# One fused kernel of a linear recurrence and an MLP: a new order of its steps on every queue, half-length MLP pieces, and two chunk results from one product

## The chip, the cores and the metric

The kernel runs on one core of a Trainium2 chip. A core has five engines that run side by side, each with an in-order instruction queue: TensorE (PE, matrix products; its weight loads are listed apart as PEld), VectorE (DVE), ScalarE (ACT), GpSimd (POOL) and SyncE (SP), which here does nothing but issue DMAs. They wait for one another by semaphores. Matrix products read SBUF and write PSUM, which is here a pool of four tiles of two banks each ("duo" in the code). The metric is the time of one execution on the device in microseconds (us).

## What is computed

The reference is a recurrence over 768 time steps for 4 batches x 8 heads with a 40 x 40 state each, and then a two-layer MLP with exact GELU over the 3072 tokens:

```python
for t in range(S):                      # S = 768
    y[:, :, t] = einsum('bhd,bhde->bhe', rt, state)
    Sa = einsum('bhde,bhe->bhd', state, at)
    state = state * wt[:, :, None, :] - einsum('bhd,bhe->bhde', Sa, bt) \
            + einsum('bhd,bhe->bhde', vt, kt)
x = y.transpose(0, 2, 1, 3).reshape(3072, 320)
out = gelu(x @ w_in) @ w_out            # w_in 320 x 2048, w_out 2048 x 320
```

All is in float32, except that the MLP's weights arrive as 64-bit floats and have to be turned into 32-bit ones on the chip, from their two 32-bit words.

## The kernel before, in words

**Chunks.** The 768 steps are cut into 12 chunks of 64 (c = 0 to 11). Within a chunk the recurrence becomes products of 64 x 64 blocks per head. With the decay of w taken into a and r (as running products) and out of b and k (as their inverses), the strictly upper parts are taken of four products: N = b.a, A = k.a, RV = v.r, and later M = sa.r. The inverse of the triangular system with N gives T (stored in `Tt`). Then, with the state S at the chunk's start:

- `make_av` (L640): av = A x v, copied to SBUF by ACT; `make_X` (L808): X = a x S, to which DVE adds av (L819).
- `make_sa` (L821): sa = T x (X + av), 40 columns per head, copied into `SM`; `make_saT` (L833): the same transposed, copied by ACT (L842, L843); `make_M` (L846): M = sa x r, masked by DVE (L575) into the other 64 columns of `SM`.
- `make_y2` (L850): r x S into the PSUM tiles `QY`, from the transposed state that `turn_state` (L912) makes; `make_QY` (L870): b x [sa | M] and k x [v | RV] added there, 104 columns at once.
- `outputs` (L879): DVE scales the 64 columns of y into `xt` (L886), adds and scales the new state (L908, L909), and SP moves parts of `xt` between partitions by eleven small DMAs (L894, L897), because 40 rows of a head don't fill 64 partitions.

Each of these steps is 32 products of a quarter of PE's array (`units`, L588), written by the helper `mm` (L110), so one line stands for all of them in the profile. A float32 product is two instructions: 32 products are x64 in a view.

**The inverse** of a chunk is made a chunk ahead. N goes to DRAM (L615) and comes back in another layout (`Nb`, L664); POOL eliminates column by column, 31 columns of a product (L672, tile `tmp`) and an addition (L674, tile `W`); the result goes to DRAM (L686, issued by POOL) and is fetched into `Tt` and `T2` (L696, L700). `corner` (L774) and `joined` (L789) put the 64 x 64 inverse together from its 32 x 32 blocks, with DVE's transpose `L` (L772) and copies of J. Chunk 0 takes another way, squarings on PE (`squares`, L712).

**Loads.** r, k, v, w, a, b of a chunk come by `fetch`, `fetch_pairs`, `load_w`, `load_r` and `load_VR` (L159 to L223), nearly all on SP's queue. For late chunks DVE's 32 x 32 transposes (L186) turn a, b, k, v and r. SP issues in program order and waits at each DMA whose buffer is in use.

**The MLP** of a chunk (`mlp`, L985) is a generator. Up to each `yield` it is one piece: four pieces of the first layer (`ph`, 20 products of 64 x 128 tiles, then a GELU by ACT at L995), and then the second layer (`po`): for chunks 0 and 1 four pieces at L1010, for later chunks four pieces of `seven` (L936), which takes seven block products in place of eight, with DVE's sums. `fill()` (L1024) takes the next piece of the oldest MLP in the list `pieces`, so the program text decides between which steps of the chunks the MLP's work stands on PE.

**The weights' conversion** (`to_float`, L312) is a handful of instructions of DVE (L319 to L328), ACT (L320) and, for some pieces, POOL (L332, L333): 10 pieces of w_in of 512 columns and 16 of w_out of 320. `first_load` and `second_load` bring the words into places that are free at that time; `convert(n)` (L338) begins the next n pieces of one queue and ends the ones before.

**The order** is written by hand: straight text for chunks 0 and 1 and the preparation of 2 and 3 (L1059 to L1242), then a loop over c = 2 to 11 (L1244) in which chunk c runs, c + 1 is prepared and c + 2 is loaded and its inverse begun. `keep(n)` puts idle products (identity times a mask, n x 128 columns) ahead of the next PSUM tile's real ones.

Of the kernel before, what the change touches and what calls it, by code (L numbers as in the profile page):

```python
# [19 lines left out]
def kernel(  # L20
# [193 lines left out]
    def load_VR(c):  # L214
        VR = turned_in.setdefault(c, {})["VR"] = VR_ring()
        for e in range(2):
            nc.sync.dma_start(out=VR[half(e)].rearrange("p g q m d -> p (g q m) d")[:, :, :D], in_=rows_of(v, c, e))
# [20 lines left out]
    st_ring = ring("st", 1, [P, 2, NP, G, HP], lambda t: t.rearrange("p e i g d -> p (e i g) d")[:, :, D:], nc.gpsimd)  # L238
# [34 lines left out]
    upper = const.tile([P, C], FP32, name="upper")  # L273
# [15 lines left out]
    part_ring, avs_ring = (ring(n, 1, [P, 2, DM + REST], lambda t: t[:, :, DM:], nc.gpsimd) for n in ("part", "avs"))  # L289
# [46 lines left out]
    queue, begun = [], []  # L336

    def convert(n, last=False):  # L338

        for _ in range(n):  # L340
            begun.append(queue.pop(0))
            next(begun[-1], None)
            if len(begun) > 1:
                next(begun.pop(0), None)
        if last:
            while begun:
                next(begun.pop(0), None)

    first_raw, second_raw = {}, {}
    late_raw = w_out_sb.rearrange("p f d -> p (f d)").bitcast(UINT32)  # L350
# [59 lines left out]
    def first_pieces(kts, part, eng):  # L410
        queue.extend(first_convert(kt, part, eng) for kt in kts)

    def second_pieces(fs, eng):
        queue.extend(second_convert(f, eng) for f in fs)
# [6 lines left out]
    decays, turned_in = {}, {}  # L421
# [5 lines left out]
    def sums(c):  # L427
        logw = raws.pop((c, "w"))
        pt = duo("wT_ps").rearrange("p e (n t) -> p e n t", t=C)
        for n in range(G * NP):  # L430
            for x in range(2):
                for e in range(2):
                    at = (2 * n + x) * D
                    mm(pt[half(x), e, n], logw[half(e), at:at + HP], cum_m[half(e), half(e)])
        cum = duo("cum")[:, :, :DM]
# [4 lines left out]
        wp = wp_ring()  # L440
        turned_in.setdefault(c, {})["wp"] = wp
        if c < NB:
            nc.scalar.activation(wp[:, :, 1:].rearrange("p (n e) t -> p e n t", e=2), pt, ACT.Exp)  # L443
        else:
            en = turned_in.setdefault(c, {})["en"] = by_batch(side("en", "kT", 1))
            for to, scale_ in ((wp[:, :, 1:].rearrange("p (g n e) t -> p g e n t", g=G, e=2), 1.0),
                               (en.rearrange("p (e g n) t -> p g e n t", e=2, g=G), -1.0)):
                for g in range(G):
                    nc.scalar.activation(to[:, g], pt[:, ::1 - 2 * g, g * NP:(g + 1) * NP], ACT.Exp, scale=scale_)
        rw = (avs_ring if c in (1, 2) else part_ring)()[:, :, :DM]  # L450
# [27 lines left out]
    def turn_a(c):  # L478
        if c < NT:
            turned_in.setdefault(c, {})["a_ps"] = flip(by_pair(raws.pop((c, "a"))), "aT_ps")  # L480
            return
        aT = turned_in.setdefault(c, {})["aT"] = work.tile([P, 2, G, NP, C], FP32, tag="aT", name="aT", bufs=2)
        turn(aT.rearrange("p e g i t -> p (e g i) t"), c, "a")
# [112 lines left out]
    direct = (0,)  # L596

    def make_N(c):
# [10 lines left out]
        if c in direct:  # L609
            return  # L610
# [8 lines left out]
    def make_RV(c, mask=True):  # L619
        t = turned_in[c]  # L620
        t["RV_ps"] = products("RV_ps", t["vT"], t["rT"], False)
        if mask:
            mask_RV(c)
# [5 lines left out]
    def make_A(c, mask=True):  # L629
        t = turned_in[c]  # L630
        t["A"] = work.tile([P, 2, G, NP, C], FP32, tag="nT", name="A")
        t["A_ps"] = products("A_ps", t["kT"], t["aT"], False)
        if mask:
            mask_A(c)
# [4 lines left out]

    def make_av(c):  # L640
        t = turned_in[c]
        av = duo("av")[:, :, :G * NP * D].rearrange("p x (g i d) -> p x g i d", g=G, i=NP)
        for g, i, x, e, q, m in units():
            mm(av[half(e ^ x), x, g, i], t["A"][half(e), x, g, i], t["VR"][half(e), g, q, m, :D])
        avs = t["avs"] = avs_ring()
        nc.scalar.copy(avs[:, :, :DM], av.rearrange("p x g i d -> p x (g i d)"))
# [161 lines left out]
    def make_X(c):  # L808
        t = turned_in[c]
        if state[0] is None:  # L810
            t["xs"] = t["avs"]
            return
        st = state[0][0]
        X = duo("X")[:, :, :G * NP * D].rearrange("p x (g i d) -> p x g i d", g=G, i=NP)
        for g, i, x, e, q, m in units():
            mm(X[half(e ^ x), x, g, i], t["aT"][half(x, D), g, i, e], st[half(x, D), e, i, g, :D])

        xs = t["xs"] = part_ring() if c == 1 else t["avs"]
        nc.vector.tensor_tensor(xs[:, :, :DM], X.rearrange("p x g i d -> p x (g i d)"), t["avs"][:, :, :DM], ALU.add)  # L819

    def make_sa(c):  # L821
        t = turned_in[c]
        xs = t["xs"]
        Tt = t["Tt"]
        sap = duo("sap")[:, :, :G * NP * D].rearrange("p x (g q a d) -> p x g q a d", g=G, q=2, a=NA)
        for g, i, x, e, q, m in units():
            at = (g * NP + i) * D
            mm(sap[half(e), x, g, q, i % NA], Tt[half(e ^ x), x, g, i], xs[half(e ^ x), x, at:at + D])
        SM = t["SM"] = SM_ring()
        copy = nc.scalar.copy if 0 < c <= NS else nc.vector.tensor_copy  # L830
        copy(SM.rearrange("p g q (a x) c -> p x (g q a) c", x=2)[:, :, :, :D], sap.rearrange("p x g q a d -> p x (g q a) d"))

    def make_saT(c):  # L833
        t = turned_in[c]
        xs, Tt = t["xs"], t["Tt"]
        pt = duo("saT_ps").rearrange("p r (i x t) -> p r i x t", i=NP, x=2)
        for g, i, x, e, q, m in units():
            at = (g * NP + i) * D
            mm(pt[half(g), e ^ x, i, x], xs[half(e ^ x), x, at:at + HP], Tt[half(e ^ x), x, g, i])
        saT = side("saT", "late", 1)  # L840
        to = saT.rearrange("p g (a x) (e t) -> p (g a) (x e) t", x=2, e=2)
        nc.scalar.copy(to[:, :, 0::3], pt[:, 0])  # L842
        nc.scalar.copy(to[:, :, 1:3], pt[:, 1])  # L843
        t["saT"] = parts(saT)

    def make_M(c):  # L846
        t = turned_in[c]
        masked(flat(t["SM"])[:, :, D:], products("M_ps", t["saT"], t["rT"], False))

    def make_y2(c):  # L850


        t = turned_in[c]
        t["QY"] = [duo("QY")[:, :, :NP * VC].rearrange("p e (i c) -> p e i c", i=NP) for g in range(G)]
        if state[0] is None:
            return
        tn = state[0][1]
        for i in range(NP):
            for e in range(2):
                for x in range(2):  # L860
                    for g in range(G):
                        mm(t["QY"][g][half(x), e, i, D:], tn[half(g, D), e, i, half(x)],
                           t["rT"][half(g, D), i // NA, 2 * (i % NA) + x, e], i == 0)
# [6 lines left out]
    def make_QY(c):  # L870
        t = turned_in[c]
        for n, (l_, r_) in enumerate(((t["nb"], t["SM"]), (t["ks"], t["VR"]))):
            for g, i, x, e, q, m in units():
                mm(t["QY"][g][half(x), e, i], columns(l_[half(e)], g, head_of(i, x)), r_[half(e), g, q, m],
                   state[0] is None and n == 0 and i == 0)
# [3 lines left out]
    def outputs(c):  # L879
# [487 lines left out]
```

## Time and profile before

| | |
|---|---|
| three runs | 714.76, 717.62, 717.79 us; median 717.62 |
| profiled execution | 722.93 us, span 721.2 us from the first to the last instruction |
| busy in the span | PE 670.3, PEld 592.0, DVE 370.7, POOL 361.1, ACT 223.0 us |
| instructions | 32844, of which PE 14826 products |
| mean granted PE clock | 0.960 |
| DMA | 74.46 MB in 287923 packets, 103 GB/s on the mean |
| first layer `ph` (L993) | 1920 instructions, 220.4 us of PE |
| second layer `po` (L946, L1010) | 1248 instructions, 201.3 us of PE |
| POOL's inverse (L672, L674) | 620 instructions, 267.5 us |

The page lists the busy time of each engine, the span in 40 equal slices (each digit is the busy share in tenths), the chain of work that ended last, and the groups of instructions by line. The trace can be asked for waits (who waited for whom), for the busy time in any stretch, and for the instructions in order of time. A busy PE is not PE at its peak: products are pipelined and their ends are modelled, so what a step costs PE is read from the start of its first product to the start of the next step's first.

### The profile page before, as it was taken

How to read it: one execution, taken by the hardware profiler on the slowest of the kernel's cores; microseconds unless marked ns; L12 is line 12 of the kernel's file. 1: busy time of each engine (PE TensorE's matmuls, PEld its weight loads, DVE VectorE, ACT ScalarE, POOL GpSimd, SP SyncE). 2: the span in 40 equal slices, each digit the busy share in tenths (PEclk: the TensorE clock that was granted, in tenths of full speed). 3: DMA queues.
4: the chain of work that ended last, by engine and by line, in shares of the span. 5: the costliest groups of instructions: out<-in, count | busy, mean ns of one | idle time of the engine just before them, and what ended most of it. 6: DMA issues, size and time to landing. Idle time of an engine off the chain costs nothing.

```text
span 721.2 us, 32844 instructions
## 1 busy us (share of the span) xinstructions
PE 670.3 (93%) x14826; PEld 592.0 (82%) x14826; DVE 370.7 (51%) x490; ACT 223.0 (31%) x311; POOL 361.1 (50%) x798
## 2 busy tenths in 40 slices
PE   7578897869999999999999999999999899999997
PEld 4567777747777889899898998898898798998987
DVE  2324889993353386384384573662761671621403
ACT  5123674444140241341332232323313323112020
POOL 5284458811841860882863844855845827800000
PEclk9775799989999999999999999999999999999999
DMA  9688437664557645757657656747737644020100
GB/s 127 119 164 153 97 87 200 132 127 96 116 115 111 131 92 90 134 101 118 130 97 132 127 92 118 140 74 128 145 62 138 132 93 73 21 54 3 28 11 18
DMA packets 287923, 74.46 MB, mean 103 GB/s; under 512 B 265736, under 2 KB 284456, under 8 KB 287784
## 3 DMA queue, kind: packets, MB, share of 16 engines
q1 hardware_dynamic: 283360, 68.20, 51.0%
q0 software_dynamic: 864, 2.36, 2.0%
q8 instruction: 116, 1.90, 1.1%
q10 hardware_dynamic: 3560, 1.80, 1.0%
q14 instruction: 23, 0.19, 0.1%
HBM read 58.69 MB, written 9.70 MB: 95 GB/s over the span
## 4 chain that ended last, share of the span: by engine, by line
PE 52%; POOL 13%; SPq 11%; DMA 10%; DVE 5%; issue 5%; ACT 3%; ACTq 1%; DVEq 0%; POOLq 0%
PE ph L993 16%; PE po L946 12%; POOL W L674 6%; POOL tmp L672 6%; PE po L1010 5%; PE QY L110 4%; PE J L110 2%; DMA Nb<-N 2%; DMA Tt<-inv 2%; DMA inv<-W 2%; SPq L181 2%; PE sq L110 2%; SPq L897 2%; SPq L178 2%; PE X L110 1%
## 5 line engine op out<-in xcount | busy, mean ns | idle before, releaser
L993 PE MATMUL ph<-xt,w_in_sb 64*128 64x256 f32 x1920 | 220.4, 381 | 0.3 <-issue 0.3
L672 POOL TENSOR_TENSOR tmp<-W,Nb 128x126 f32<-128x126 f32 (+22 forms) x310 | 131.9, 425 | 157.6 <-DMA Nb<-N 134.6
L993 PEld LDWEIGHTS ph<-xt,w_in_sb 64*128 64x128 f32 x1920 | 182.7, 187 | 23.3 <-issue 1.7
L674 POOL TENSOR_TENSOR W<-W,tmp 128x126 f32<-128x126 f32 (+22 forms) x310 | 135.6, 438 | 24.3
L995 ACT ACTIVATE gt<-ph 128x1024 f32<-128x1024 f32 x48 | 49.1, 1023 | 153.0 <-PE ph L993 152.9
L946 PE MATMUL po<-w_out_sb,gt 128*128 128x160 f32 x640 | 92.2, 302 | 0.1
L946 PEld LDWEIGHTS po<-w_out_sb,gt 128*128 128x128 f32 x640 | 87.5, 190 | 2.4 <-DVE gt L966 0.4
L186 DVE STREAM_TRANSPOSE aT<-a_pairs 128x1024 f32<-128x1024 f32 x9 | 11.2, 1246 | 62.9 <-DMA a_pairs<-in_a_dram 62.9
L1010 PE MATMUL po<-w_out_sb,gt 128*128 128x320 f32 x128 | 38.5, 459 | 2.2 <-ACT wpT L443 2.2
L1010 PEld LDWEIGHTS po<-w_out_sb,gt 128*128 128x128 f32 x128 | 25.2, 201 | 13.3 <-ACT wpT L443 2.4
L802 DVE COPY Tt<-J 32x512 f32<-32x512 f32 x9 | 6.2, 689 | 52.8 <-ACT Tt L802 52.8
L786 ACT COPY Js<-J 128x256 f32<-128x256 f32 x11 | 4.1, 370 | 88.7 <-PE J L110 88.7
L946 PE MATMUL po<-extra,half 128*128 128x160 f32 x192 | 28.5, 303 | 0.0
L998 DVE TENSOR_TENSOR half<-gt 128x1024 f32<-128x1024 f32 x10 | 12.4, 1244 | 28.0 <-ACT gt L995 28.0
L946 PEld LDWEIGHTS po<-extra,half 128*128 128x128 f32 x192 | 26.4, 190 | 0.4
L575 DVE TENSOR_TENSOR SM<-M_ps,upper 128x1024 f32<-128x1024 f32 x12 | 14.5, 1204 | 21.2 <-PE M_ps L110 21.2
L320 ACT ACTIVATE conv<-conv,rebias 128x320 uint32<-128x320 uint32 (+1 forms) x26 | 16.1, 623 | 27.8 <-DVE conv L319 22.0
L995 ACT ACT_TABLE_LOAD x10 | 12.8, 1283 | 37.2 <-PE ph L993 37.1
L946 PE MATMUL po<-extra,gt 128*128 128x160 f32 x160 | 23.4, 299 | 0.0
L946 PEld LDWEIGHTS po<-extra,gt 128*128 128x128 f32 x160 | 22.3, 190 | 0.0
L950 DVE TENSOR_TENSOR os<-os,po 128x160 f32<-128x160 f32 x40 | 12.6, 316 | 18.6 <-PE po L946 12.5
L961 ACT COPY os<-po 128x160 f32<-128x160 f32 x10 | 2.9, 292 | 59.1 <-PE po L946 50.2
(224 smaller groups left out, 1144.2 us busy)
## 6 DMA issues: line engine op xcount, KB each, us to landing
Nb<-N SPq DMA_DIRECT2D x20, 256.0 KB
VR<-in_v_dram SPq DMA_DIRECT2D x24, 160.0 KB
out_dram<-os SPq DMA_DIRECT2D x48, 80.0 KB
b_rows<-in_b_dram SPq DMA_DIRECT2D x22, 160.0 KB
k_rows<-in_k_dram SPq DMA_DIRECT2D x22, 160.0 KB
N<-N SPq DMA_DIRECT2D x44, 64.0 KB
Tt<-inv SPq DMA_DIRECT2D x44, 64.0 KB
a_pairs<-in_a_dram SPq DMA_DIRECT2D x18, 144.0 KB
```

What stands on the lines that cost most here:

```text
L110: nc.tensor.matmul(o, lhsT, rhs, start=first, stop=True, skip_group_check=True)
L178: eng.dma_start(out=to[:, e::2], in_=pairs[rows, :, cols])
L181: eng.dma_start(out=to, in_=pairs[rows, :, cols])
L320: nc.scalar.activation(power, power, ACT.Relu, bias=rebias, scale=8.0)
L575: nc.vector.tensor_tensor(to, pt, upper.unsqueeze(1).to_broadcast([P, 2 * G * NP, C]), ALU.mult)
L672: eng.tensor_tensor(t, W[:, :rows, j:j + 1].to_broadcast([P, rows, rest]), Nb[:, j:j + 1, j + 1:].to_broadcast([P, rows, rest]), ALU.mult)
L674: eng.tensor_tensor(W[:, :rows, j + 1:], W[:, :rows, j + 1:], t, ALU.add)
L897: eng.dma_start(out=xt[own + n * i:own + n * (i + 1), NP], in_=xt[other + REST:other + D, i])
L946: nc.tensor.matmul(po[:, n, :DM // 2], l_[:, f], r_[:, f], start=f == 0, stop=f == NF // 2 - 1)
L993: nc.tensor.matmul(ph[:, x, s], w_in_sb[half(x), kt, p * P:(p + 1) * P], xt[half(x), kt], start=kt == 0, stop=kt == NK - 1)
L995: nc.scalar.activation(gt[:, 4 * q:4 * q + 4].rearrange("p (x s) t -> p x s t", x=2), ph, ACT.Gelu)
L1010: nc.tensor.matmul(po[:, g], gt[:, f, g * P:(g + 1) * P], w_out_sb[:, f], start=f == 0, stop=f == NF - 1)
```

## The change

1. **sa and M from one product.** `make_av` now takes A x [v | RV] (104 columns), and `make_X` adds a x [S | y2] to it in the same PSUM tiles (`XA`), so the tile holds [X + av | its product with r]. ACT and DVE copy it into `SM`. `make_sa` takes T x SM, 104 columns, and DVE multiplies by a mask whose first 40 columns are one: that gives [sa | M]. `make_saT` and `make_M` are gone. For it y2 has to be there ahead of X: `make_y2` writes a PSUM tile of its own, and ACT copies it into the state's tile, now 104 columns wide.
2. **The output** is split. `add_state` adds `QY` to the state's tile [S | y2] (DVE, 104 columns), `to_x` makes `xt`, `next_state` scales the state into a tile of its own, from which ACT copies it back.
3. **Half-length MLP pieces.** Every piece is cut in two (the last product of `seven` is alone as before), so a chunk has 15 or 16 pieces in place of 8. Two sums of `seven` stand one piece earlier.
4. **Conversions** are named and begun and ended one by one (`first`, `second`, `end`) in place of the queue; all w_out loads are issued by SP.
5. **The order** of steps, loads and conversions is new throughout: straight text for chunks 0 to 3 and the preparation of 4 and 5, a loop for c = 4 to 9, straight text for 10 and 11. `keep` gives way to `warm`, seven calls with 16 idle products of 128 columns in all, six of the calls in chunks 0 and 1. N's store (`send_N`) is a step of its own, and `sums` is cut into `sums` and `sums_rows`.

The core of the diff:

```diff
+    def both_pairs(name):
+        return [duo(name)[:, :, :NP * VC].rearrange("p x (i c) -> p x i c", i=NP) for _ in range(G)]
     def make_av(c):
-            mm(av[half(e ^ x), x, g, i], t["A"][half(e), x, g, i], t["VR"][half(e), g, q, m, :D])
-        nc.scalar.copy(avs[:, :, :DM], av.rearrange("p x g i d -> p x (g i d)"))
+        t["XA"] = both_pairs("XA")
+            mm(t["XA"][g][half(e ^ x), x, i], t["A"][half(e), x, g, i], t["VR"][half(e), g, q, m], i == 0)
     def make_X(c):
-            mm(X[half(e ^ x), x, g, i], t["aT"][half(x, D), g, i, e], st[half(x, D), e, i, g, :D])
-        nc.vector.tensor_tensor(xs[:, :, :DM], X.rearrange(...), t["avs"][:, :, :DM], ALU.add)
+                        mm(XA[g][half(e ^ x), x, i], t["aT"][half(x, D), g, i, e], st[half(x, D), e, i, g], False)
+        for g, copy in enumerate((nc.scalar.copy, nc.scalar.copy if 0 < c <= NS else nc.vector.tensor_copy)):
+            copy(SM[:, g], XA[g].rearrange("p x i c -> p i x c"))
     def make_sa(c):
+        S = both_pairs("S")
+            mm(S[g][half(e), x, i], Tt[half(e ^ x), x, g, i], SM[half(e ^ x), g, i, x])
+            nc.vector.tensor_tensor(SM[:, g], S[g].rearrange("p x i c -> p i x c"),
+                                    pass_upper.unsqueeze(1).unsqueeze(1).to_broadcast([P, NP, 2, VC]), ALU.mult)
-    def make_saT(c):
-    def make_M(c):
     def make_y2(c):
+                        mm(Y2[half(x), g, e, i], tn[half(g, D), e, i, half(x)],
+                           t["rT"][half(g, D), i // NA, 2 * (i % NA) + x, e])
+        nc.scalar.copy(st.rearrange("p e i g c -> p (e i) g c")[:, :, :, D:], Y2.rearrange("p g e i t -> p (e i) g t"))
+    def add_state(c):
+                nc.vector.tensor_tensor(given[g][:, :, :, cols], t["QY"][g][:, :, :, cols], given[g][:, :, :, cols], ALU.add)
+    def next_state(c):
+            nc.vector.tensor_tensor(apart[:, :, :, g, :D], given[g][:, :, :, :D], fb, ALU.mult)
+        nc.scalar.copy(new.rearrange("p e i g c -> p (e i g) c")[:, :, :D],
+                       apart.rearrange("p e i g d -> p (e i g) d")[:, :, :D])
     def mlp(c):
+                if s == 0:
+                    yield
```

The loop after, whole but for the assignment of n = c + 1 and n2 = c + 2 (a line of several steps here is several lines there):

```python
    for c in range(4, 10):
        fill(); corner(c); fill(); fill(); joined(c)
        load_a(n2); load_w(n2); fill(); turn_v(n); make_sa(c)
        turn_a(n2); load_r(n2); fill(); fill(); make_QY(c)
        fetch_pairs(n2, "b_turned", ...); logs(n2); turn_r(n2)
        add_state(c); next_state(c)
        fetch(n2, "k", ...); fetch_pairs(n2, "k_turned", ...); load_v(n2)
        to_x(c); pieces.append(mlp(c)); fill()
        scale_b(n); fetch(n2, "b", ...); make_A(n); fill(); sums(n2); fill()
        make_RV(n); turn_b(n2); fill(); fill()
        mask_A(n); scale_a(n2); mask_RV(n); fill()
        make_N(n2); send_N(n2); fetch_inverse(n); turn_state(); turn_k(n2); sums_rows(n2)
        steps = start_inverse(n2, nc.gpsimd); fill(); inverse_columns(steps, 8)
        make_av(n); turn_corner(n); fill(); load_VR(n2); make_y2(n)
        run(steps); fill(); make_X(n); scale_k(n2); store_inverse(n2, (nc.gpsimd,))
```

In the loop before, the same steps of chunk c stand in the order corner, make_X, joined, make_sa, make_saT, (loads of n2), turn_a(n2), make_y2, make_M, make_QY, outputs, make_A(n), sums(n2), turn_state, fetch_inverse(n), make_av(n), turn_b(n2), make_RV(n), make_N(n2) with N's store and Nb's load, the inverse, turn_corner(n), with eight `fill()` among them.

The order of chunks 0 and 1 after, shortened to the steps that the text speaks of:

```python
    fetch(0, "k", ...); first_load(False, 1, ...)
    logs(0); sums(0); ...; logs(1); sums(1); ...; make_N(0); next(zero)   # zero: the squarings of chunk 0
    first_load(False, 0, ...); turn_b(1); make_N(1); send_N(1); warm(4); ...; next(zero)
    inv1 = start_inverse(1, ...); first(1, 0, nc.gpsimd); first(2, 0, nc.gpsimd); next(zero); warm(4)
    first(0, 0, nc.vector); ...; next(zero); turn_k(0); next(zero); end((0, 0)); turn_v(0); make_A(0)
    ...; next(zero); ...; turn_r(0); turn_k(1); ...; make_RV(0); ...; first(3, 0, nc.vector); turn_v(1)
    corner_direct(0, ...); mask_RV(0); ...; make_av(0); ...; make_X(0); ...; second(0, nc.vector); make_A(1)
    ...; joined_direct(0); ...; first(4, 0, nc.gpsimd); ...; make_sa(0); make_QY(0); fetch_inverse(1); ...
    first(1, 1, nc.gpsimd); ...; first(2, 1, nc.gpsimd); next_state(0); ...; to_x(0); sums(2); ...; corner(1); ...
    turn_state(); first(4, 1, nc.vector); second(2, nc.vector); make_av(1); ...; make_y2(1); second(1, nc.vector)
    turn_v(2); make_X(1); ...; turn_b(2); ...; joined(1); ...; make_N(2); first(0, 1, nc.gpsimd); make_sa(1)
    ...; send_N(2); fill(); fill(); ...; make_QY(1); ...
```

Between make_QY(1) and make_X(2) stand 15 `fill()`, the remaining thirteen conversions of w_out one after another, and the preparation of chunks 2 and 3.

## The prediction

> **What bounds the kernel now.** I read the summary of busy time and its 40 slices first, then the busy time by stretches, the waits, the chain of work that ended last, and the timeline of each engine for the first 170 us and for one chunk in the middle.
>
> ```profile
> PE 670.3 (93%) x14826; PEld 592.0 (82%) x14826; DVE 370.7 (51%) x490; ACT 223.0 (31%) x311; POOL 361.1 (50%) x798
> ...
> PE   7578897869999999999999999999999899999997
> ...
> DVE  2324889993353386384384573662761671621403
> ...
> PEclk9775799989999999999999999999999999999999
> ```
>
> A slice is 18 us. From the tenth on TensorE (PE) is full, so there only PE's own work and its stalls count. Before that PE is 50 to 90% busy at a clock of 0.5 to 0.9: this is the ramp, the first 170 us. DVE has much idle time in the first 80 us and none at 100 to 160. The stretches (busy us of PE, PEld, DVE, ACT, POOL; then clock, DMA share, GB/s) say it in numbers:
>
> ```profile
> 60.00:80.00 20.00, 17.06 (x468) 15.82 (x468) 11.34 (x17) 13.15 (x20) 6.38 (x14) 0.50 0.78 141
> ...
> 100.00:120.00 20.00, 15.69 (x388) 13.82 (x388) 19.38 (x23) 11.94 (x18) 17.38 (x26) 0.95 0.59 156
> ...
> 331.40:386.00 54.60, 53.03 (x1266) 48.15 (x1266) 30.49 (x38) 15.90 (x23) 30.16 (x68) 1.00 0.65 117
> 386.00:435.00 49.00, 48.63 (x1172) 44.07 (x1168) 27.39 (x33) 15.53 (x22) 29.83 (x68) 1.00 0.65 117
> ```
>
> The last two are whole chunks, from one X to the next. Without idle time a chunk is 50.2 us of PE; from 229.9 to 641.3 eight chunks took 411.4 us where PE needs 7 x 50.2 + 48.2 = 399.6 (the eighth prepares nothing). So 11.8 us are stalls. The chain names their source: a cycle through POOL, DMA and SP's queue.
>
> ```profile
> 436.00 5.56 DMA Nb<-N
> ...
> 477.80 3.35 DMA inv<-W
> ...
> 481.57 2.23 DMA Tt<-inv
> ...
> 485.82 3.43 DMA N<-N
> ...
> 489.93 4.08 DMA Nb<-N
> ```
>
> (Start, duration.) From one load of Nb to the next are 53.9 us, more than PE's 50.2. N of the next chunk lay ready at 479.3 (its mask on DVE), but its store was issued at 484.3, behind the fetch of the inverse in SP's queue. The other stall is the mask of M behind a transpose that waits for a DMA:
>
> ```profile
> PE QY L110 <- DVE SM L575: 12.4, 7, 3.7
> ```
>
> **The sum, against the profiled execution: 722.9 us (span 721.2 and 1.7 around it).** The three timed runs have a median of 717.6, so part of the stalls that I take away may be smaller there; I predict the absolute time.
>
> *1. PE work per chunk.* Start to start in the timeline, a step of 32 products costs 0.93 to 1.07 us at 40 or at 64 columns alike (sap 0.96, y2 0.98, wT 0.93), and 1.47 at 104 (QY, first half). saT and M go: 2 x 0.95 = -1.9. av, X and sa grow to 104 columns: 3 x (1.47 - 0.96) = +1.5. Against this stands the interleaving. Four ph pieces on end are 17.47 us (4.37 each), one alone between steps is 4.52; po pieces on end are 4.35, alone 4.54. So a run of pieces costs 0.15 to 0.19 us more than its pieces, and the last step of a run about 0.10 more than one in the middle. Before there are 7 runs of pieces per chunk, after it 11: 4 x 0.27 = +1.1. Net +0.7 (between 0 and +1.0); over ten chunks, those of the ramp left out, **+6 us** (0 to +10). The product saved is spent on switching.
>
> The Trainium skill has a rule against this part: "TensorEngine Tiling (Array Packing)", Key Properties, says that changing the tiling mode drains the engine. The trace agrees: the 0.15 to 0.19 above are pieces beside steps of smaller tiles. Without the rule, by -1.9 and +1.5 alone, this term would be -4.
>
> *2. DVE and ACT per chunk.* DVE loses the add of X (0.82), the copy of sa (0.82), the mask of M (1.20) and two state additions (0.96): 3.8. It gains half the copy of XA, two masks of S and two wider additions, all 128x832. No row has that size; 640 columns take 0.82 and 1024 take 1.20 to 1.22, so each is between, near 1.0: 5.0. ACT loses 0.74 and 1.18, gains copies of XA (0.9), of Y2 (1.03, as the copy of tn) and of the state (0.74): +0.75. DVE has 20 us idle per chunk and ACT 35, so +1.2 and +0.75 are hidden, except where one ends just before PE needs it. The tightest: Y2's copy must be done before X, with one half piece (2.27) over 1.03; and the two masks of S (2.0) before QY, under two half pieces (4.5). If a cover fails, PE pays 1 to 2 us per chunk.
>
> *3. Stalls from chunk 3 on.* In the new loop N is sent before the inverse is fetched, so its store (2.0 issue, 3.4 landing, less gaps: 5.0 from 484.3 to 489.3) leaves the cycle: 53.9 - 5.0 = 48.9 us, under PE's 50.9. DVE now has the masks of S ahead of the transpose of the next a, so that wait is not ahead of QY. SP still issues some 65 DMAs per chunk, 45 us of 51; the new order makes it wait for QY (k's buffer) and for N, and it issues without a gap from QY to VR, some 30 us, then has about 5 us to spare. Three us of stalls I leave: **-9 us** (-11 to +4, if one wait of 2 us per chunk is new).
>
> *4. The ramp.* Marks of before: fourth square of chunk 0 at 47.4, QY of chunk 0 at 76.7, X of chunk 1 at 87.8, QY of chunk 1 at 117.8 (two whole MLP pieces issued by then), X of chunk 2 at 155.5 (five pieces).
> - Squares: between the third and the fourth, PE has kT, A, vT and rT queued (38.2 to 47.4). After, only kT (1.7): 6 us sooner. Chunk 1's w, b and a now come before chunk 0's N, but ACT does its logarithm without the wait for nT: the first square starts about 3 us sooner too. RV, turns and vT(1) stand before the corner afterwards, so little of the two reaches it. An MB of w_in words loaded ahead delays chunk 1's N and its inverse on POOL by 2 to 3 us.
> - Chunk 0: saT (2.26), M (2.46) and their waits (0.7, 1.3) go at half clock; sa and av widen by 2.4: -4. Ahead of X of chunk 1 the state now goes through flip 1.0, copy 1.05, y2 1.1, copy 1.03 and a state copy 0.74: +5. X of chunk 1 stays near 88 to 90.
> - X to QY of chunk 1 took 30 us with DVE full: conversions of w_in at 3 us each stood before the masks. After, eight of ten pieces of w_in are begun before X(1), in DVE's idle time; between X and QY stand the copies (1), joined, turns and N (5), sa with masks (4) and two half pieces (4.5): 14 to 15 us, QY near 104.
> - Then DVE bounds: 13 conversions of w_out at 2.65 (525 + 638 + 610 + 474 + 399 ns) = 34.4, and 16 for masks, scalings and transposes: 50 us; PE has 15 half pieces (34) and 10 of steps. X of chunk 2 near 104 + 3 + 50 = 157, with 17 half pieces done where before had 10: 7 x 2.27 - 1.5 = **-14.4 us**. From the rows it lies between -26 (rival C) and +12 (rival A).
> - Fillers: the `keep` products go (4.0 us in six rows), the `warm` ones come: 16 units of 128 columns at 1.1 per four = 4.4. Even.
> - Eight w_out loads move from ACT's queue to SP's: about 8 us of issue, ACT free of it. The end of the kernel stays: a last MLP of 33 us at full PE, and 4.2 us.
>
> Sum: 722.9 + 6 - 9 - 14.4 = **705.5 us**.
>
> **Rivals.**
> A. *Slower: DVE's queue in the ramp.* A conversion waits for its load with chunk masks queued behind it, and all loads now stand in SP's one queue, which itself waits (the load of piece 14 behind the store of chunk 2's inverse, so behind POOL). Two issues (1.2) and a landing of 2 to 3 us, exposed by 2.0 for each of 13: 26 us, 731 us. It decides from 17.4 / 13 = 1.3 us each. For it: SP's waits for DVE are long already. Against: at 117 to 163 sixteen conversions ran almost without a gap (1.1 us idle before L319). 0.18.
> B. *The cycle stays.* If the fetch of the inverse still holds up the load of Nb (it is still ahead of it), or POOL's 35 us stretch, the 9 us remain: 714.5. 0.14.
> C. *The clock comes back.* From 24 to 80 us PE lost busy time times (1 - clock) = 16 us by the stretches of 4 us; a denser queue with fillers may keep it up. Three quarters are on the path: -12, 693.5. For: PE waits least where the clock is 1.0, at 80 to 112. Against: at 60 to 80 it was 85% busy at 0.50. 0.13. ("TensorE: Matmul & The Clock Gate", Part 1, of the Trainium skill, ties the half clock to idle windows of some 3.4 us; the trace disagrees, since no wait of PE from 24 to 60 us is over 2.2.)
> The forecast, 698 to 712: 0.55.
>
> **Range and chances.** 690 to 723 takes in C, B and the lower part of A and leaves out under 2 in 10. 0.5% of 717.6 is 3.6 us, about what a measurement tells from no change: faster is below 714.0, slower above 721.2. Faster: forecast, C and a little of B, 0.70. Same: the rest of B, 0.12. Slower: A, 0.18.
>
> **What would show it.** QY of chunk 1 near 104 and X of chunk 2 near 157 with 17 half pieces before it; chunks of 50.5 to 51 us at almost no idle time, so each a little longer in PE work than before; no PE wait for SM's mask; Nb to Nb set by PE. Wrong if DVE at 60 to 104 idles on loads, if corner waits for L, or if ph waits for xt: a chunk's first ph piece stands seven pieces behind its QY, some 23 us, and xt needs about 19.

## The result and the profile after

The changed kernel takes **694.3 us** (median of four runs, 692.65 to 694.72); the kernel before, run beside it, 716.2. The ratio is **0.969, with a 95% interval from 0.966 to 0.972**. The direction was right and the time lies in the range, but the change is 22 us, where the forecast had 11 to 12 by the medians: it is about twice as large as I predicted.

The page of the changed kernel, profiled at 692.65 us (busy time; then the 40 slices of 17.3 us; then the shares of the chain that ended last):

```profile
PE 662.9 (96%) x13292; PEld 574.7 (83%) x13292; DVE 387.4 (56%) x493; ACT 235.6 (34%) x311; POOL 381.9 (55%) x796
...
PE   7778899889999999999999999999999999999997
...
DVE  0667768953536683772872863863863852623303
...
PEclk9888899998999999999999999999999999999999
...
PE 84%; POOL 4%; DMA 3%; SPq 3%; issue 2%; DVE 2%; ACT 1%; ACTq 0%; DVEq 0%; POOLq 0%
```

DVE is now busy from the second slice on, where it stood at 2 to 4 tenths, and the clock of the ramp no longer falls to 5. PE is 84% of the chain; before it was 52%. The same by stretches (busy us of PE, PEld, DVE, ACT, POOL; then clock, DMA share, GB/s):

```profile
60.00:80.00 20.00, 16.28 (x525) 14.59 (x524) 15.03 (x25) 13.24 (x20) 14.83 (x24) 0.74 0.87 171
80.00:100.00 20.00, 18.77 (x522) 16.48 (x516) 12.91 (x24) 13.11 (x19) 2.56 (x2) 1.00 0.60 110
100.00:120.00 20.00, 20.00 (x308) 17.15 (x301) 16.32 (x34) 8.78 (x14) 11.10 (x25) 1.00 0.93 208
```

At 100 to 120 PE has no idle time (it had 4.3) and DVE has some (it had 0.6). From 314.5 to 569.5, from X of chunk 5 to X of chunk 10, are five chunks of exactly 51.0 us, without idle time on PE. From here on the kernel is bound by PE's own work.

Where the time went, from profile to profile (spans 721.2 and 690.9, so 30.3 us): the marks are the starts of X, and a half piece of MLP that is done sooner or later is counted at 2.27 us.

| stretch | before, us | after, us | gain at equal work | forecast |
|---|---|---|---|---|
| start to X(2) | 155.5 | 154.3, with 7 half pieces more | 17.1 | 14.4 |
| X(2) to X(4), chunks 2 and 3 | 125.1 | 99.5 | 5.2 | -0.1 |
| X(4) to X(10) | 311.7 | 315.7 | 5.1 | 3.2 |
| X(10) to the end | 128.9 | 121.4 | 3.0 | -0.1 |

The forecast's column spreads its +6 over chunks 2 to 11 and its -9 over chunks 3 to 10.

How much of the last three rows is waiting, and how much PE's own work, can be read from the same stretches, before:

```profile
155.50:280.60 125.10, 122.51 (x2458) 101.98 (x2448) 66.66 (x89) 35.72 (x49) 56.73 (x135) 0.97 0.57 108
280.60:592.30 311.70, 303.30 (x7112) 275.08 (x7104) 168.80 (x205) 93.16 (x132) 186.47 (x408) 0.99 0.63 115
592.30:721.20 128.90, 124.09 (x2116) 113.40 (x2104) 38.78 (x56) 21.42 (x32) 29.92 (x65) 1.00 0.17 34
```

and after:

```profile
154.30:253.80 99.50, 99.49 (x1978) 82.42 (x1982) 55.79 (x60) 30.98 (x40) 62.20 (x132) 0.97 0.66 116
253.80:569.50 315.70, 315.70 (x6431) 278.55 (x6421) 190.84 (x215) 104.02 (x136) 198.22 (x411) 1.00 0.63 117
569.50:690.90 121.40, 116.87 (x1810) 107.00 (x1808) 40.03 (x56) 20.84 (x31) 29.98 (x65) 1.00 0.13 27
```

PE's idle time, the stretch less its busy time, was 2.6, 8.4 and 4.8 us and is 0.0, 0.0 and 4.5 (in the last stretch nearly all of it lies behind the last product). So 2.6, 8.4 and 0.3 us of the gain are waits that went. The rest is PE's work at equal pieces, which changed by -2.6, +3.3 and -2.7 us.

### The profile page after: what moved, and what is told of

Same layout as the page of the kernel before. It is cut to its first block, busy times and chain, and to the rows that moved or that the text cites. A ratio compares the mean times of both kernels' runs of the same rounds, so it can differ in the third digit from the quotient of the medians.

```text
span 690.9 us, 29686 instructions
## 1 busy us (share of the span) xinstructions
PE 662.9 (96%) x13292; PEld 574.7 (83%) x13292; DVE 387.4 (56%) x493; ACT 235.6 (34%) x311; POOL 381.9 (55%) x796
## 3 DMA queue, kind: packets, MB, share of 16 engines
q0 software_dynamic: 864, 2.36, 1.8%
## 4 chain that ended last, share of the span: by engine, by line
PE 84%; POOL 4%; DMA 3%; SPq 3%; issue 2%; DVE 2%; ACT 1%; ACTq 0%; DVEq 0%; POOLq 0%
PE ph L999 29%; PE po L951 23%; PE XA L110 5%; PE QY L110 5%; PE po L1020 4%; PE S L110 3%; PE J L110 2%; POOL W L680 2%; POOL tmp L678 2%; DMA w_out_sb<-in_moe_w_in_dram 2%; SPq L163 2%; PE RV_ps L110 2%; PE A_ps L110 2%; PE tn_ps L463 1%; PE Y L110 1%
## 5 line engine op out<-in xcount | busy, mean ns | idle before, releaser
L999 PE MATMUL ph<-xt,w_in_sb 64*128 64x256 f32 x1920 | 225.0, 384 | 0.0
L999 PEld LDWEIGHTS ph<-xt,w_in_sb 64*128 64x128 f32 x1920 | 181.8, 188 | 25.3 <-issue 0.8
L678 POOL TENSOR_TENSOR tmp<-W,Nb 128x126 f32<-128x126 f32 (+22 forms) x310 | 139.3, 450 | 102.3 <-DMA Nb<-N 78.8
L680 POOL TENSOR_TENSOR W<-W,tmp 128x126 f32<-128x126 f32 (+22 forms) x310 | 145.9, 471 | 24.3
L834 DVE TENSOR_TENSOR SM<-S,upper 128x832 f32<-128x832 f32 x24 | 23.5, 1019 | 19.5 <-PE S L110 19.5
L825 DVE COPY SM<-XA 128x832 f32<-128x832 f32 x10 | 10.2, 1024 | 34.5 <-PE XA L110 34.5
L848 ACT COPY st<-Y 128x1024 f32<-128x1024 f32 x11 | 11.1, 1010 | 45.7 <-PE Y L110 45.7
L778 DVE STREAM_TRANSPOSE L<-Tt 128x512 f32<-128x512 f32 x11 | 7.8, 706 | 33.4 <-DMA Tt<-inv 33.4
L918 ACT COPY turned<-tn_ps 128x1024 f32<-128x1024 f32 x11 | 11.1, 1013 | 43.1 <-PE tn_ps L463 43.0
L668 POOL MEMSET W<- 128x512 f32 x10 | 5.3, 530 | 34.9 <-DMA inv<-W 34.8
```

Source lines behind the costliest of these rows:

```text
L678: eng.tensor_tensor(t, W[:, :rows, j:j + 1].to_broadcast([P, rows, rest]), Nb[:, j:j + 1, j + 1:].to_broadcast([P, rows, rest]), ALU.mult)
L680: eng.tensor_tensor(W[:, :rows, j + 1:], W[:, :rows, j + 1:], t, ALU.add)
L834: nc.vector.tensor_tensor(SM[:, g], S[g].rearrange("p x i c -> p i x c"), pass_upper.unsqueeze(1).unsqueeze(1).to_broadcast([P, NP, 2, VC] ...
L999: nc.tensor.matmul(ph[:, x, s], w_in_sb[half(x), kt, p * P:(p + 1) * P], xt[half(x), kt], start=kt == 0, stop=kt == NK - 1)
```

## The experiments

**Theory** (the prediction's): the gain comes from the order, that is from conversions moved into DVE's idle time in the ramp, and from the stalls of the loop's cycle through POOL, DMA and SP; the single product and the halves are near even. **Rivals**: the single product carries it (R1), the half-length pieces do (R2), or the clock does, by the fillers (R3), that is by the idle products of `warm`. The kernel before runs beside every group, at medians of 715.1 to 718.5 us.

### The ramp

*Without the later fillers.* The edit (the expectation below says four times 1; the kernel has three, so 11 units go, and `warm(3)` and `warm(2)` at the start stay):

```diff
-    warm(4)        # twice
-    warm(1)        # three times
```

> The changed kernel without its later warm() products (4, 4 and four times 1 in units of 128 columns; the first 3 and 2 stay, which the kernel before had as keep). Theory: fillers are even, they cost 3 us of PE on a path that DVE and POOL set in good part: 691 to 697 us. Rival, the better clock of the first 80 us (0.91 and 0.74 where before had 0.74 and 0.50) is the fillers' doing: the clock in 40 to 80 us falls back towards 0.5 to 0.7 and the time is 700 to 706 us.

693.5 us, ratio 0.969 (0.963 to 0.974): no difference from the changed kernel. The clock at 20 to 80 us was 0.74, 0.83 and 0.74 where the changed kernel has 0.91, 0.91 and 0.74, and nothing of it reaches the end. R3 falls for these eleven units.

*The squares.* v's turn, A and r's turn of chunk 0 ahead of the fourth square again:

```diff
     turn_k(0)
-    next(zero)
     end((0, 0))
     turn_v(0)
     make_A(0)
+    load_r(0)
+    mask_A(0)
+    turn_r(0)
+    next(zero)
...
     run(zero)
-    mask_A(0)
-    load_r(0)
-    turn_r(0)
```

> The changed kernel with v's turn, A and r's turn of chunk 0 put back ahead of the fourth square, as in the kernel before. Theory: the fourth square comes at 46 in place of 40, but RV, the turns of chunk 1 and the corner stand behind it anyway, so little reaches X of chunk 1: 694 to 698 us. Rival, the squares' chain is the path of chunk 0 and what it loses reaches the end: 699 to 703 us.

695.5 us, ratio 0.971 (0.965 to 0.978). The rival is out; the squares' place is worth some 1 us, which these intervals don't separate from nothing. X of chunk 1 came at 91.8 in place of 86.3, X of chunk 2 at 158.1 in place of 154.3, but four other runs, which are the changed kernel up to X of chunk 1, have the two marks at 87.2 to 90.1 and at 154.6 to 155.8, so most of the first difference may be no effect of the edit.

*The conversions.* The first try moved the conversions and their loads:

```diff
-    first_load(False, 1, ...)      # ahead of logs(0)
...
-    first_load(False, 0, ...)      # behind the first square
...
-    first(1, 0, nc.gpsimd); first(2, 0, nc.gpsimd)
...
-    first(0, 0, nc.vector)
...
     turn_k(0)
...
+    first_load(False, 1, ...); first_load(False, 0, ...)
...
-    first(3, 0, nc.vector)
...
     make_X(0)
+    first(1, 0, ...); first(2, 0, ...); first(0, 0, ...); first(3, 0, ...)
...
```

> The changed kernel with the first four conversions of w_in and their two loads put back to where the kernel before had them (loads after turn_k(0), conversions after X of chunk 0). Theory: about 4 x 2.8 = 11 us of DVE move from its idle time before 75 us to the full stretch behind X of chunk 1; QY of chunk 1 comes at 105 to 112 in place of 99, X of chunk 2 some 6 to 11 us later: 700 to 706 us. Rival, DVE's total up to X of chunk 2 is not the bound and the gain of the ramp lies in the clock and the squares: 693 to 697 us.

710.7 us, ratio 0.992 (0.988 to 0.995): 16 us of the 22 are gone. Two things spoil the reading: r's load stood behind w_in's words (RV waited 8.8 us for the copy of rT), and the words of w_out's first block landed on words of w_in that were not yet converted, so one part of w_in is false here. The second try leaves the loads of w_in in place:

> The changed kernel with all loads of w_in where it has them and only the first four conversions of w_in late, one after the other behind A of chunk 1, sa, QY and xt of chunk 0, as in the kernel before (the first four words of w_out, which take the same room, are loaded and converted behind them). Theory: about 11 us of DVE go from its idle time before 75 us to the full stretch after X of chunk 0; QY of chunk 1 at 103 to 110 in place of 99, X of chunk 2 5 to 10 us later, the end 698 to 705 us. Rival, the first of the two runs on this cost 16 us by the load of r that stood behind w_in's words, not by DVE: 693 to 697 us.

707.6 us, ratio 0.987 (0.982 to 0.993). Here the second block of w_out was written on words of the first ahead of their conversion, so the first block is false. The third mends that order; its core, the conversions one after the other as before had them (`second(0)` also moves, ahead of `make_y2(1)`):

```diff
     make_A(1)
+    first(0, 0, nc.vector); end((0, 0))
...
     make_sa(0)
+    first(1, 0, nc.gpsimd)
     make_QY(0)
+    first(2, 0, nc.gpsimd)
...
     to_x(0)
+    first(3, 0, nc.vector); end((1, 0)); end((2, 0)); end((3, 0))
+    second_load(0, ...); second_load(2, ...); second_load(4, ...); second_load(1, ...)
```

> The changed kernel with the first four conversions of w_in late, behind A of chunk 1, sa, QY and xt of chunk 0 as in the kernel before, and the first conversions of w_out, whose words take the same room, behind them in their own order; all loads of w_in stand where the changed kernel has them. Theory: DVE's idle time before 75 us is lost, the two earlier tries gave 13 and 16 us: X of chunk 2 at 164 to 170, the end 704 to 709 us. Rival, the false order of w_out's words made the wait: 694 to 700 us.

711.6 us, ratio 0.989 (0.982 to 0.996): 17 us over the changed kernel by the medians, 14 by the ratios, 19 by the profiles, and more than I expected. X of chunk 1 comes at 105.3 (86.3), X of chunk 2 at 173.0 (154.3); behind it the chunks are those of the changed kernel, 51.0 to 51.1 us. One stretch of it, and PE's waits at 70 to 125 us (total, times, longest):

```profile
80.00:100.00 20.00, 10.05 (x232) 8.91 (x232) 13.37 (x19) 10.19 (x14) 7.11 (x6) 0.66 0.47 96
```

```profile
PE aT_ps L463 <- issue: 7.0, 1, 7.0
PE XA L110 <- ACT st L848: 4.6, 1, 4.6
PE J L110 <- DVE L L778: 2.9, 1, 2.9
```

PE is busy for 10 us of 20 where the changed kernel has 18.8. DVE is busy for 25.3 us at 20 to 75 us where the changed kernel has 38.0, so some 13 us of its work have left its idle time. The 7.0 us ahead of aT end at 87.4, while DVE makes xt behind two of the late conversions (78.9 to 85.8), so I read them as a wait for DVE. But not all of the loss is that work: DVE also stands idle, ahead of a conversion of w_out (start, duration; SPq is SP issuing).

```profile
95.50 5.16 SPq L401 DMA_DIRECT2D w_out_sb<-in_moe_w_out_dram  x8
...
100.81 0.33 DVE L321 TENSOR_SCALAR conv<-w_out_sb 128x320 uint32<-128x320 uint32 x1 [6.96 <-PE vT_ps L110]
...
104.17 0.99 ACT L848 COPY st<-Y 128x1024 f32<-128x1024 f32 x1
```

The row names a product as what ended these 7.0 us; in the second try the same conversion waits 7.0 us for the DMA of w_out's words, and here SP issues that load only at 95.5. ACT's copy `st`, for which X of chunk 1 waits, stands behind ACT's step of that conversion. So the place of four conversions, with the w_out words that follow them in the same room, is worth about the whole gain of the ramp; up to 7 us of it may be the later words alone, which no run parts from the rest.

### The half-length pieces

*Whole pieces everywhere.* The edit lets `fill` count halves and issue two at a time:

```diff
     def fill(n=1):
+        owed[0] += n
+        while pieces and owed[0] >= size of the next piece:   # 2, or 1 for the last of seven
+            issue it whole; owed[0] -= size
```

> The changed kernel with whole MLP pieces: every fill() is counted, and a piece of two halves is issued as soon as two are owed, so a piece stands at most one half later than in the changed kernel and never earlier. Theory of the prediction: the halves cost PE about 0.27 us for each additional run of pieces, 4 per chunk, so whole pieces give back about 1 us per chunk, 690 to 685 us by itself; where a cover fails (the copy of Y2 ahead of X, the masks of S ahead of QY) 1 to 2 us per chunk come on top, so between 684 and 700. Rival, the half-length pieces carry the gain (their finer spread is what leaves PE without a wait): the stalls of before return, 11.8 us from chunk 3 on and some 5 in the ramp, 705 to 715 us.

701.2 us, ratio 0.979 (0.972 to 0.985), between the two expectations, and each holds in its part. In the loop a chunk falls to 49.7 to 51.1 us. But from X(2), at 154.6 as in the changed kernel, to X(5) it takes 168.2 us in place of 160.2, and from X(10) to the end 126.1 in place of 121.4; one half piece less is done at X(2), none at X(5) and X(10). PE's waits at 155 to 206 and at 206 to 260 us:

```profile
PE XA L110 <- ACT st L848: 6.0, 1, 6.0
PE QY L110 <- DVE SM L834: 1.6, 2, 1.0
...
PE wT_ps L110 <- ACT w_tile L425: 1.7, 1, 1.7
```

The changed kernel has one wait of 3.2 in the first stretch and none in the second. *Whole pieces in the loop alone* follow from this:

```diff
+    by_two[0] = True
     for c in range(4, 10):
...
+    by_two[0] = False
     scale_b(11)
```

> The changed kernel with half pieces up to chunk 3 and at the end, and whole pieces in the loop (chunks 4 to 9). The run with whole pieces everywhere took 49.8 to 51.2 us per chunk in the loop in place of 51.0, but came to the loop 6 to 8 us later and left it with 2 us more. Theory (halves cost four runs of pieces of 0.27 us per chunk, and pay only where PE would wait): 6 x 1.0 = 6 us less than the changed kernel, 686 to 690 us. Rival, the later start and end of the run with whole pieces are the price of the loop's own shift: 694 to 698 us.

689.3 us, ratio 0.963 (0.957 to 0.969), the lowest of all. The theory holds, with 5.0 of the 6 us by the medians: span 687.1 against 690.9, X(4) to X(10) 311.2 against 315.7. The two intervals of the ratio touch, so it is the traces' chunks that show it. The price of a switch can be read from the chain of the changed kernel (start, duration), with half pieces on their own:

```profile
410.77 2.36 PE ph L999 x20
413.13 1.09 PE Y L110 x64
414.22 2.36 PE ph L999 x20
416.58 1.59 PE XA L110 x64
418.17 2.36 PE ph L999 x20
420.53 0.68 PE J L110 x50
```

and from the timeline of the run with whole pieces, where the same steps stand closer:

```profile
315.80 1.66 PE L110 MATMUL XA<-VR,A 64*64 64x104 f32 x64
317.28 1.11 PE L110 MATMUL Y<-rT,turned 40*64 40x64 f32 x64
318.32 4.59 PE L999 MATMUL ph<-xt,w_in_sb 64*128 64x256 f32 x40
322.84 1.66 PE L110 MATMUL XA<-st,aT 40*64 40x104 f32 x64
```

From start to start, a half piece between two steps takes 2.36 (413.13 - 410.77), and a whole one 4.52 (322.84 - 318.32), 0.20 less than two halves; the Y step takes 1.09 between two pieces and 1.04 in front of one when a step is ahead of it, XA 1.59 and 1.48. With the fillers taken out as well:

> The changed kernel with whole pieces in the loop and without its later warm() products. Theory: the two edits add up, 6 us and 0 to 1 us less than the changed kernel: 686 to 690 us. Rival, without the fillers the clock of the ramp falls now and then: 690 to 696 us with a wider spread.

691.4 us, ratio 0.964 (0.958 to 0.971): not apart from the one before, and no gain from taking out the fillers.

### The stalls of the loop

*The store of N behind the fetch of the inverse*, in the new order:

```diff
         make_N(n2)
+        fetch_inverse(n)
         send_N(n2)
-        fetch_inverse(n)
```

> The changed kernel with one swap in the loop (chunks 4 to 9): the inverse of the next chunk is fetched ahead of N's store of the chunk after, as in the kernel before. Theory: the cycle through POOL, DMA and SP's queue is again 53.9 us in place of 48.9, over PE's 51.0, so each of the six chunks may lose up to 2.9 us: 700 to 711 us, and Nb to Nb becomes longer than 51. Rival, the stalls left because DVE's masks of S now stand ahead of the transpose of a, and the store's place is hidden: 694 to 696 us.

702.6 us, ratio 0.981 (0.975 to 0.988): 8 us lost. Chunks go from 51.0 to 53.0 to 54.4 us from the third of the loop on, as the theory says. Its chain of work at 425 to 486 us holds nothing of PE (start, duration; POOL's columns and SP's issues are left out):

```profile
425.51 5.01 DMA Nb<-N
...
468.09 3.35 DMA inv<-W
471.85 3.26 DMA Tt<-inv
...
477.39 1.98 DMA N<-N
...
480.02 4.18 DMA Nb<-N
```

From load to load of Nb are 54.5 us, and the store of N stands behind Tt again. This is the cycle of the prediction.

*The reverse swap in the kernel before.* There the fetch moves behind N's store:

```diff
             turn_state()
-            fetch_inverse(n)
             make_av(n)
...
             make_N(n2)
+            fetch_inverse(n)
             steps = start_inverse(n2, nc.gpsimd)
```

> The kernel before with one move in its loop: the inverse of chunk n is fetched behind N's product and store of n + 1 in place of ahead of av. Theory: N's store leaves the cycle of 53.9 us, the stalls of POOL and SP go, and the wait for SM's mask (7.4 to 12.4 us in all) may stay: 705 to 713 us, chunks near 51. Rival, the fetch now holds up the loads behind it or the corner waits for Tt: 715 to 725 us.

Ratio 1.011 (1.002 to 1.019): slower. My expectation fell. *The turn of the next a* behind the mask of M, in the kernel before:

```diff
-            turn_a(n2)
-            fetch_pairs(n2, "b_turned", ...)
         fill()
         make_y2(c)
         make_M(c)
+            turn_a(n2)
+            fetch_pairs(n2, "b_turned", ...)
```

> The kernel before with one move in its loop: DVE's transpose of the next a (and the load that waits for it) stands behind M and its mask in place of ahead of them. Theory: the wait of QY for SM's mask (7.4 us in chunks 3 to 10) goes, chunks come down to 50.3 to 51.5 us, 5 to 8 us less than before: 708 to 713 us. Rival, the later turn delays the next load, nT and N, so the wait comes back at the inverse: 715 to 722 us.

Ratio 1.002 (0.997 to 1.008): nothing. *Both at once*:

> The kernel before with both moves of its loop at once: the inverse fetched behind N's store, and the transpose of the next a behind the mask of M. Theory that the two waits are the whole stall and each hides the other: chunks of 50.3 to 51 us, 706 to 713 us. Rival, in the old order every step behind the late one is as tight (A's mask, L's turn), so the wait moves on: 716 to 726 us, with PE waiting for L or for A.

730.4 us, ratio 1.016 (1.009 to 1.023). The rival is right: the wait moves on. PE waits 7.9 us in seven places for L, and the chain (start, duration) says why:

```profile
433.29 1.14 DVE N L575
...
437.00 2.37 DMA Tt<-inv
...
439.46 0.72 DVE L L772
...
440.32 0.74 PE J L110 x48
```

In the old order N is masked at 433.3 to 434.4, some 6 us before the corner (J at 440.3); in the first profile of before N's product starts at 476.7 and J at 484.8, 8 us later. If the fetch waits for N's store, Tt lands at 439.4 and the corner waits for it; if it doesn't, the store waits for the fetch and POOL's cycle grows. In the new order N's product starts at 404.0, ahead of av, y2, X and four half pieces, and J at 420.5 (the chain above): 16.5 us later, which leaves room for store, fetch and turn. So, by these traces, the swap needs the longer way from N to the corner; the new order with a short way was not run.

*The turn of the next a ahead of sa and its masks*, in the new order:

```diff
         turn_v(n)
+        turn_a(n2)
         make_sa(c)
-        turn_a(n2)
```

> The changed kernel with the transpose of the next a (which waits for its load) ahead of sa and its masks in the loop. Theory: the masks of S come later by the turn and the wait for the load, 1.2 to 4 us, against a cover of 4.5 us under two half pieces: 694 to 700 us. Rival, DVE's order was the cause of the old stalls by itself: chunks of 52 to 54 us, 702 to 712 us.

695.6 us, ratio 0.967 (0.962 to 0.973), chunks of 51.0 to 51.1 and no wait of PE from 254 to 571. DVE's order by itself is not what took the stalls away.

### The single product alone

The kernel before with the new functions for av, X, sa, y2 and the output, in its own order and with whole pieces:

```diff
             make_A(n)
-            make_av(n)
...
             make_RV(n)
+            mask_A(n)
+            mask_RV(n)
...
             turn_k(n2)
+            make_av(n)
+            make_y2(n)
         fill()
         corner(c)
         make_X(c)
...
         make_sa(c)
-        make_saT(c)
-        make_M(c)
```

> The kernel before with the functions of the changed one (sa and M from one product, split output, the copy of Y2), in the order, the loads and the conversions of the kernel before, with whole pieces; av, y2 and X stand together at the end of a chunk's preparation, since the tiles of XA can't be held for long. Theory: the fusion alone is nearly neutral for PE (two steps of 0.95 us go, three widen by 0.5 us each) and takes away DVE's mask of M behind a transpose (12.4 us of waits in seven chunks): 704 to 714 us. Rival, the single product is where the gain comes from: 690 to 700 us. Third: without the new order the wider copies stand bare between X and sa, and it gets slower than 720 us.

745.5 us, ratio 1.039 (1.030 to 1.048). In this placement R1 falls, and so does my own forecast for it. By the profiles half of the loss lies in the ramp (X(2) at 167.3 in place of 155.5) and half between X(2) and X(10) (449.0 us in place of 436.8). PE's waits from 240 to 670 us:

```profile
PE po L951 <- ACT en L444: 8.3, 7, 2.3
PE po L951 <- ACT st L848: 8.0, 7, 1.1
```

A second-layer piece waits for ACT's copies `en` and `st`, which it doesn't read. ACT reads there the PSUM tiles of w's sums and of Y2, so I read it as a wait for one of the four tiles, two of which XA holds from av to X. This is one placement of the new functions in the old order, and perhaps not its best: it shows that the product brings no gain by being put in, not what it could bring.

### The kernel before once more

> The kernel before once more, for the spread of its marks from one execution to the next: if the 722.9 us of the first profile were that execution's own, chunks from 230 to 641 us are shorter here or the ramp ends sooner; if they are the kernel's, X of chunk 2 is at 155 and a chunk takes 51.4 us on the mean again, and the end is within 3 us of it.

722.8 us, X(2) at 155.1 and X(3) to X(11) in 412.3 us: the profile that I started from was no stray one. The profiled executions of the kernel before are both some 5 us over the medians of its timed runs, the changed kernel's is not; I have no run that says why.

## Why the prediction was right and wrong

*What bounds the kernel*: right. The ramp gave 17 us, the stalls from X(4) to X(10) 8.4 (311.7 less 303.3 of busy PE), and with them gone PE is the bound.

*Step 1, PE's work per chunk, is the step that failed: its term was mis-sized, because a count that holds in the loop was charged to all ten chunks.* The sum has +6 us. By the rows above, PE's work at equal pieces changed by -2.6, +3.3 and -2.7, so by -2.0 us from X(2) to the end: 8 of the 13 us that the profiles gained beyond the forecast.

In the loop the term is right. From X(4) to X(10) it is +3.3 where I had 3.6; a loop chunk is 51.0 where before needed 50.2 without its idle time (+0.8, forecast +0.7), and whole pieces bring it to 49.7 in the best chunks, so the halves cost 1.3 where I had 1.1 and the product saves 0.5 where I had 0.4. But the four additional runs of pieces per chunk are there alone. Counted in the timelines, X(4) to X(10) has 67 runs where before had 42, X(2) to X(4) has 17 where before had 15, and X(10) to the end 12 as before: 27 more, where I charged 40. (A run is pieces on end without a step between them.) The 13 that never came are 3.5 us at my price of 0.27, and the price is borne out: with whole pieces in the loop X(4) to X(10) has 43 runs, 24 fewer, and PE is busy for 308.9 us in place of 315.7, so 0.28 each. Two smaller parts: from X(2) on the steps of the single product (XA and S) take 47.0 us from start to start where the five old ones took 52.8, so it saved 5.9 where I had 4; and the N and nT of one chunk, 2.1 us in X(2) to X(4) before, now stand ahead of X(2). Together 7.5 of the 8; the remainder is open.

*The halves* do not explain these two stretches by a better cover: there were only 2.6 and 0.3 us of waits to win from the kernel before. But the new order needs them, which I credited with nothing. With whole pieces everywhere it takes 11.9 us more than with whole pieces in the loop alone (701.2 and 689.3; 10.9 by the ratios): 8 us from X(2) to X(5), less 2.3 for the half piece not yet done at X(2), and 5 behind X(10). Up to X(5) a piece of 4.5 us comes too coarse: a short cover is missing ahead of X and QY, and they wait for ACT's state (6.0 us) and DVE's masks (1.6 us). Behind X(10) the longest wait is 2.3 us, ahead of J, and the profile names nothing for it. In the loop, where PE never waits, halves are a pure cost. Whether the old order would have gained by halves was not tried.

*Step 2*: right. DVE's and ACT's additions are hidden; PE waits for neither in the loop.

*Step 3, the stalls*: right in its cause, and too small. The store of N in the cycle is worth 8 us in the loop (expected 6 to 17). I had taken off 9 us of stalls; 11.3 us of PE's idle time went from X(2) on. Wrong was the second half of the reason, DVE's masks ahead of the turn of a: that order is worth nothing measurable in the new kernel. And what I didn't see is that the swap alone doesn't work: it made the old order 1% slower. What made it possible, as I read the traces, is that the corner moved behind av, y2 and X.

*Step 4, the ramp*: the main step was right. QY of chunk 1 at 104 was forecast and came at 99.3, X of chunk 2 at 157 and came at 154.3, with 17 half pieces as forecast. Of 17.1 us I had 14.4. Taking back the early conversions costs 14 to 19 us, up to 7 of them perhaps by the later words of w_out, and the squares about 1.

*The base*: I made the sum against the profiled 722.9 us and forecast 17.4 less. By the two profiles it is 30.3, by the medians 21.9. The distance from 705.5 to 694.3 is made of step 1 (8.0), the ramp (2.7) and the stalls (2.3); the profiled execution of the changed kernel is 1.6 under its median, which takes 1.6 back. That the time still lies in the range is in part luck: the range was made wide for other reasons, C's better clock among them.

*The rivals.* A: DVE did wait for loads, 12.2 us in all at 60 to 154, but 6.3 of them just ahead of X(2), and X(2) came at 154.3 all the same; PE was full at 100 to 120. B: the cycle left. C: the clock did come back in part (at 20 to 60 us 0.91 for 0.74, at 60 to 80 us 0.74 for 0.50), and the time is near the one given for C, but for another reason: without the fillers the clock is lower again and the time the same. What of the ramp the clock gave is inside the 17 us and was not measured apart. The trace after speaks against the half clock after idle windows of some 3.4 us ("TensorE: Matmul & The Clock Gate", Part 1, of the Trainium skill) as the trace before did: 0.74 at 60 to 80 us, with PE busy for 16.3 of 20 and no wait of it over 2.4 us from 44 to 80.

## What to carry to other kernels

A price that is paid per switch has to be counted stretch by stretch: four more runs of pieces per chunk were right in the loop and wrong in the chunks around it. Cut long filler work into halves where the engine would wait for the step that they cover, and leave it whole where it doesn't: in this order the cut saved 11 to 12 us outside the loop, and cost 1.3 us per chunk inside. Before a store or a fetch is moved in a cycle, measure the way from its producer to the step that needs the fetched data, since the swap that gains 8 us here, with 16.5 us between them, cost 1% in the order with 8. In a ramp, look for an engine that is idle early and full later, and move its work there before anything else.

## What was not expected of the hardware

- X of chunk 1 comes at 86.3 to 90.1 us in five kernels that are the same up to there, at clocks of 0.74 to 0.91 in 60 to 80 us, and X of chunk 2 at 154.3 to 155.8 in all of them: what the ramp differs by at the first mark is mostly gone at the second. Which engine takes it up was not measured.
